# Attention-output transposes on half of the array, and eight other edits, in a kernel of sliding-window attention and RWKV channel mix

## Chip, cores and metric

One core of a Trainium2 chip runs the whole kernel. The metric is the device time of one launch in microseconds (us). Engines are named as in the profile: PE (TensorE matmul), PEld (its weight load), DVE (VectorE), ACT (ScalarE), POOL (GpSimd) and SP (SyncE). Lines such as L652 are lines of the kernel before.

## What is computed

```python
# q, k, v: (8, 8, 576, 64) f32: batch, heads, sequence, head size
scores = q @ k.T / 8
rel = pos[:, None] - pos[None, :]
mask = (rel >= 0) & (rel < 128)                    # window of 128, causal
attn = softmax(where(mask, scores - slope[h] * abs(rel), -1e9))   # slope[h] = 2**-(h+1)
x = (attn @ v) with the heads side by side         # (8, 576, 512)

xp = x moved down by one row, zeros in the first
xk = mu_k * x + (1 - mu_k) * xp
xr = mu_r * x + (1 - mu_r) * xp
v = relu(xk @ w_k) ** 2 @ w_v                      # w_k 512x1024, w_v 1024x512
out = sigmoid(xr @ w_r) * v                        # w_r 512x512, f32 result
```

## The kernel before

**A planner writes the order.** Every piece of work is added to a `Plan` (L33) as a node with an engine or a choice of engines, a duration from a formula, dependencies, buffers that it takes (`Hold`) and frees, and a priority. `Plan.run` (L89) plays these durations through and emits the instructions in the order that comes out. On the chip each engine then runs its own list strictly in that order. Attention work of group `g` of batch `b` is given the time `(4b + g - A[engine]) * SLOPE` in `rank` (L283), channel-mix work the sum of the PE time of the channel mix before it. So a larger `A` means that the engine takes attention earlier relative to the channel mix. `paced` (L742) holds back attention that would run too far ahead. `XRL` and `XD` delay the mixing of `xr` and of late batches.

**Attention.** The 8 batches have 4 groups of 2 heads each (a pair of heads is a group). For batches 1 to 4, q and k arrive as bf16 over POOL's DMA queue in `cb`, are transposed on PE (L935, eight 128x128 tiles) and copied from PSUM to `qk` by ACT. Batches 5 to 7 are transposed by DMA from SP's queue (L410) instead. `scores` (L531) multiplies q with k: the contraction is the 64 of the head size, so the two heads of a group sit in the upper and the lower 64 rows of the array, at the same time (12 matmuls at L559 for one group). ACT takes the exponential (L570), DVE multiplies by `mask` (L583), or, for the first groups, the bias is added by matmuls with `sid` and `dist` (L546). `attend` (L589) multiplies with v (18 matmuls at L614); DVE takes the reciprocal of the sums (L620) and normalizes into `xu` (L625). `out_t` (L641) transposes the five 128-row tiles of `xu` back on PE (L652, `xu` as the weights, the identity streaming through in 128 columns), and ACT copies 576 columns into `xt` (L529, the helper `copy_any`). `shift` (L661) makes the difference with the row before (L678) and mixes it into `xk` and `xr` (L685). Batches 6 and 7 go back by DMA (L697).

**Channel mix.** `channel_mix` (L750) works on at most 512 rows: eight blocks of `xk @ w_k` (L765), ReLU on ACT (L772), square on DVE or ACT (L738, L736), then, for each 128 rows, `xr @ w_r` (L783), tanh on ACT (L790), eight matmuls with `w_v` (L799), the product on DVE into one of four `ot` tiles (L804), and a DMA out from SP (L820). The last tile of all is done in column pieces of 384 and 128, both in one PSUM bank.

**Start.** Batch 0 is cut in two: `part` 0 is its first 256 rows, `part` 1 the rest. The f32 q and k of part 0 are loaded by six DMAs from SP (L422) into `stage`, cast to bf16 by ACT (L855), transposed on PE (L867) and copied to `qk` by ACT or DVE (L873). Part 1 and all the rest come over POOL's queue, casting, in the order `LOADS`: v tiles 0 and 1, half of `w_k`, k and q of part 1, the 64 rows at the end of q and k (`ts`, the tails), v tiles 2 and 3, the other half of `w_k`, batch 1, `w_r`, `w_v`. The tails are transposed at L716 and copied to `tt` by two DVE copies. `mask` is made by eight ACT exponentials (L900). 90 matmuls on zeros (L520) fill PE while there is nothing else to do.

**PSUM** has two double banks (`duo`, class `p2`) for scores and attention, and four single ones (`uno`, class `p1`) for everything else; the channel mix and the transposes share these four.

```python
A = {PE: 8.75, ACT: 4.50, DVE: 6.75, VIR: 0}
return {e: ((k - A[e]) * SLOPE,) + tuple(prio) for e in A}     # attention
return {e: (prio[1],) + tuple(prio) for e in A}                # channel mix
```

## Time and profile before

| | us |
|---|---|
| launch, median of 4 runs (lowest to highest) | 239.11 (238.65 to 240.27) |
| the profiled execution's own time | 238.65 |
| its span, first to last instruction | 236.9 |
| PE busy, of the span | 228.4 (96%) |
| DVE busy | 186.8 (79%) |
| ACT busy | 164.8 (70%) |
| POOL busy | 102.2 (43%) |
| `xt` copies of 576 columns on ACT, 20 of them, each | 0.647 |
| `mask` exponentials on ACT, 8 of them, each | 0.443 |

The profiled execution is also the fastest of the four; 1.75 us of its time lie outside the span. An engine's busy time says little by itself here, since matmul ends are modelled and shares are averages over a start, a long middle and an end; the prediction reads them by stretch. The granted TensorE clock is 1.00 in every stretch.

### The profile page before, as it was taken

To read this page: it belongs to the slowest core of one execution; us is meant where nothing else is said; L and a number is where in the kernel's file an instruction comes from. 1 tells how busy PE (TensorE), PEld (TensorE's weight loads), DVE (VectorE), ACT (ScalarE), POOL (GpSimd) and SP (SyncE) were. 2 spreads that over 40 slices of the span, in tenths; PEclk is the share of its full clock that TensorE was granted. 3 is DMA by queue.
4 is the path that set the end of the run, shared out by engine and by line. 5 is a ranking of instruction groups with operands and counts; after the bars stand their busy time and mean duration, and the time that the engine had idled before them with its cause. 6 is when DMAs were issued, how large, how long until landed. Compare 5 with 4: busy or idle time off the path is not lost.

```text
span 236.9 us, 5786 instructions
## 1 busy us (share of the span) xinstructions
PE 228.4 (96%) x2255; PEld 140.6 (59%) x2255; DVE 186.8 (79%) x420; ACT 164.8 (70%) x283; POOL 102.2 (43%) x128
## 2 busy tenths in 40 slices
PE   8969999999999999999999999999999999999993
PEld 7556676575675856565565674555565744455562
DVE  6676946899699998999999988975699955964342
ACT  4768999779998895977785776855783726326260
POOL 8778985598794893179257626000000000000000
PEclk9999999999999999999999999999999999999999
DMA  8999999999999999999999999972331214121212
GB/s 146 198 151 167 155 154 187 155 167 201 181 138 169 152 144 172 151 122 168 205 152 95 161 207 174 79 148 91 77 115 44 91 45 144 44 90 47 86 46 89
DMA packets 136491, 31.44 MB, mean 133 GB/s; under 512 B 127112, under 2 KB 131984, under 8 KB 136464
## 3 DMA queue, kind: packets, MB, share of 16 engines
q0 software_dynamic: 110992, 16.26, 110.9%
q1 hardware_dynamic: 25472, 14.82, 28.1%
q8 instruction: 17, 0.28, 0.5%
q14 instruction: 10, 0.08, 0.2%
HBM read 33.56 MB, written 9.44 MB: 182 GB/s over the span
## 4 chain that ended last, share of the span: by engine, by line
PE 84%; ACT 6%; DMA 4%; POOL 3%; issue 1%; DVE 0%; POOLq 0%; DVEq 0%; ACTq 0%
PE uno L799 27%; PE uno L765 25%; PE uno L783 13%; PE duo L614 7%; PE duo L559 6%; DMA ts<-in_k_dram 4%; PE uno L935 3%; PE uno L652 3%; POOL qx L381 1%; ACT at L570 1%; ACT qk L529 1%; ACT rl L772 1%; ACT xt L529 1%; PE uno L716 1%; ACT mask L900 1%
## 5 line engine op out<-in xcount | busy, mean ns | idle before, releaser
L799 PE MATMUL uno<-wv_sb,kk 128*128 128x512 bf16 (+2 forms) x296 | 72.1, 374 | 0.7 <-DVE ot L804 0.7
L570 ACT ACTIVATE at<-duo 128x1024 bf16<-128x1024 f32 (+2 forms) x68 | 65.3, 992 | 8.5 <-PE duo L559 8.5
L765 PE MATMUL uno<-xk,wk_sb 128*128 128x256 bf16 (+2 forms) x416 | 69.6, 314 | 0.2 <-ACT rl L772 0.2
L772 ACT ACTIVATE rl<-uno 128x256 bf16<-128x256 f32 (+2 forms) x104 | 47.9, 486 | 16.5 <-PE uno L765 14.8
L765 PEld LDWEIGHTS <-wk_sb 128*128 128x128 bf16 x416 | 38.9, 98 | 21.7 <-issue 0.3
L738 DVE TENSOR_TENSOR kk<-rl 128x256 bf16<-128x256 bf16 (+2 forms) x94 | 30.4, 339 | 15.5 <-ACT rl L772 14.4
L799 PEld LDWEIGHTS <-kk 128*128 128x128 bf16 x296 | 26.6, 98 | 26.4 <-issue 0.9
L384 POOL DMA_DIRECT2D vs<-in_v_dram x32 | 28.4, 901 | 27.2 <-PE duo L614 24.7
L790 ACT ACTIVATE rs<-uno 128x512 bf16<-128x512 f32 x36 | 22.2, 617 | 24.8 <-PE uno L783 24.6
L583 DVE TENSOR_TENSOR at<-at,mask 128x1024 bf16<-128x1024 bf16 x54 | 36.1, 678 | 4.1 <-ACT at L570 4.0
L783 PE MATMUL uno<-wr_sb,xr 128*128 128x512 bf16 x144 | 37.0, 379 | 0.0
L804 DVE SCALAR_TENSOR_TENSOR ot<-rs,uno 128x512 f32<-128x512 bf16 (+2 forms) x37 | 24.6, 666 | 14.1 <-PE uno L799 10.6
L406 POOL DMA_DIRECT2D cb<-in_k_dram x28 | 24.8, 897 | 9.1 <-DMA wv_sb<-in_moe_w_v_dram 4.1
L685 DVE SCALAR_TENSOR_TENSOR xk<-dl,mu_sb,xt 128x576 bf16<-128x576 bf16 (+2 forms) x36 | 26.7, 744 | 0.2
L406 POOL DMA_DIRECT2D cb<-in_q_dram x28 | 24.7, 906 | 4.5 <-PE uno L935 1.5
L685 DVE SCALAR_TENSOR_TENSOR xr<-dl,mu_sb,xt 128x576 bf16<-128x576 bf16 (+2 forms) x36 | 26.4, 743 | 0.0
L614 PEld LDWEIGHTS <-at 128*128 128x128 bf16 x576 | 21.9, 98 | 6.1 <-issue 0.3
L529 ACT COPY xt<-uno 128x576 bf16<-128x576 bf16 (+2 forms) x28 | 16.2, 582 | 9.2 <-PE uno L652 9.2
L783 PEld LDWEIGHTS <-xr 128*128 128x128 bf16 x144 | 13.5, 98 | 14.2
L529 ACT COPY qk<-uno 128x1024 bf16<-128x1024 bf16 (+1 forms) x20 | 18.1, 942 | 3.1 <-PE uno L935 2.7
L678 DVE TENSOR_TENSOR dl<-xt 128x576 bf16<-128x576 bf16 (+2 forms) x36 | 15.0, 422 | 5.3 <-ACT xt L529 4.9
L614 PE MATMUL duo<-vs,at 128*128 128x65 bf16 x448 | 19.1, 194 | 0.0
(64 smaller groups left out, 217.3 us busy)
## 6 DMA issues: line engine op xcount, KB each, us to landing
out_dram<-ot SPq DMA_DIRECT2D x35, 256.0 KB, 2.5
vs<-in_v_dram POOLq DMA_DIRECT2D x32, 128.0 KB, 6.5
cb<-in_q_dram POOLq DMA_DIRECT2D x28, 128.0 KB, 7.3
cb<-in_k_dram POOLq DMA_DIRECT2D x28, 128.0 KB, 6.5
wk_sb<-in_moe_w_k_dram POOLq DMA_DIRECT2D x2, 512.0 KB, 8.1
wv_sb<-in_moe_w_v_dram POOLq DMA_DIRECT2D x2, 512.0 KB, 10.6
ts<-in_q_dram POOLq DMA_DIRECT2D x8, 64.0 KB, 6.6
ts<-in_k_dram POOLq DMA_DIRECT2D x8, 64.0 KB, 6.5
```

The costliest lines, as they stand in the source:

```text
L384: return dma(POOL, 256, issue_t(1024), lambda e: nc.gpsimd.dma_start(out=vs_buf[h.idx][:, j, :, 0:D], in_=v[b, :, 128 * j:128 * j + 128].r ...
L406: return [dma(POOL, 256, issue_t(1024), lambda e, r=r: nc.gpsimd.dma_start(out=cb_buf[h.idx][:, i, r], in_=src[:, :, r]), [g]) for r in ra ...
L529: (nc.scalar.copy if e == ACT else nc.vector.tensor_copy)(out=out, in_=in_)
L570: lambda e, ah=ah, w=w, hp=hp: nc.scalar.activation(out=ah(), in_=two(hp)[:, :, 0:w], func=AF.Exp, scale=float(scale)), (), [hp])
L583: nc.vector.tensor_tensor(out=a, in0=a, in1=m, op=ALU.mult)
L614: nc.tensor.matmul(a[:, hl, t - t0], lhsT=at[:, lo:lo + 128], rhs=vs[:, u, 2 * g + hl, :] if u < NF else tvb[:, 2 * g + hl], start=(u == u ...
L685: lambda e: nc.vector.scalar_tensor_tensor(out=buf[hk.idx][:, g, e0 + c0:e0 + c1], in0=dls(), scalar=mu[:, g:g + 1], in1=xc(1), op0=ALU.mu ...
L738: nc.vector.tensor_tensor(out=out, in0=in_, in1=in_, op=ALU.mult)
L765: nc.tensor.matmul(one(hp)[:, 0:n], lhsT=wk_sb[:, po, 128 * fo:128 * fo + 128], rhs=xk_buf[hx.idx][:, po, c0:c1], start=(po == 0), stop=(p ...
L772: a = op(ACT, act_t(n), [s], pr, lambda e, hp=hp, hr=hr: nc.scalar.activation(out=rl_buf[hr.idx][:, 0:n], in_=one(hp)[:, 0:n], func=AF.Rel ...
L783: nc.tensor.matmul(one(hp), lhsT=xr_buf[hx.idx][:, po, 128 * c:128 * c + 128], rhs=wr_sb[:, po], start=(po == 0), stop=(po == NPO - 1))
L799: nc.tensor.matmul(one(hv)[:, a:b], lhsT=kk_buf[hk.idx][:, fo, o:o + 128], rhs=wv_sb[:, fo, a:b], start=(fo == 0), stop=(fo == NFO - 1))
```

## The change

What it does, part by part:

1. The transposes of the attention output of batches 1 to 5 (20 groups) use 64 of the 128 rows at a time: `out_some` instead of `out_t`. Each 128x128 tile becomes two weights of 64x128, one in each half of the rows, with 64 columns of the identity streaming; the two halves write to two PSUM banks, and two ACT copies (320 and 256 columns) take the place of one of 576. The transposes of q and k stay as they were (`QM = 0`).
2. The planner knows the cost of a change between 128-row and 64-row work on PE (`SWITCH`), takes 64-row work first while PE is in that mode (`pe_key`), and models the DMA queues in slices (`fab`).
3. A fifth `ot` tile (`NO = 5`); the early buffer `dl0` now lies in it.
4. The last tile's second column piece has a PSUM bank of its own, and its DMA goes out from ACT's queue. The seven tiles before the last are sent in two DMAs each (`n_split`).
5. Start: k of groups 0 to 3 is loaded from ACT's queue, q from SP's; groups 2 and 3 are transposed by PE in f32, straight from `stage`, without a cast; the casts of groups 0 and 1 go to DVE; the copies to `qk` go to ACT alone, batch 0's copies to `xt` to ACT or DVE. The first v load waits for k of group 0, and the causal cut of `dist` comes before it on POOL.
6. `mask` comes from eight PE matmuls and two ACT exponentials of 1024 columns.
7. The tails are copied to `tt` by one DVE copy of 512 columns, in a new order of columns.
8. All squares of the channel mix go to DVE.
9. Pacing: `A` from 8.75/4.50/6.75 (PE/ACT/DVE) to 10/3/5, `SLOPE` from 4.7 to 4.6, `XRL` from 3 to 4, `XD` from 4 to 7, `OTL` from 5 to 1.5.

```diff
+    SWITCH = 0.095
...
+    def pe_key(self, n, rows):
+        key = n.prio["PE"] if isinstance(n.prio, dict) else n.prio
+        if rows == 64 and n.rows[0] == 64:
+            return (-1e8,) + tuple(key)
+        if rows == 128 and n.lazy:
+            return (key[0] + self.wait,) + tuple(key[1:])
+        return tuple(key)
...
-                    cand.sort(key=lambda n: n.prio[e] if isinstance(n.prio, dict) else n.prio)
+                    if e == "PE":
+                        cand.sort(key=lambda n: self.pe_key(n, rows))
...
+                    if e == "PE":
+                        if n.rows[0] != rows:
+                            n.dur = dur = dur + self.SWITCH
+                        rows = n.rows[1]
...
-    XD = 4
-    OTL = 5.0
+    XD = 7
+    OTL = 1.5
...
-    NO = 4
+    NO = 5
+    WAIT = 0.0
+    QM = 0
+    OM = 1
...
-        return (DVE, ACT) if order < 3 else (DVE,)
-
-    XT0 = (ACT,)
-    QK0 = (ACT, DVE)
-    CAST = (ACT,)
+        return (DVE,)
+
+    XT0 = (ACT, DVE)
+    QK0 = (ACT,)
+    CAST = (DVE,)
+    FT = (2, 3)
+    KQ = ACT
+    VCUT = True
+    XTT = range(8, B)
+    MMASK = True
+    VDEP = 1
+    TCOST = 1.5
+    KLAST = 1
...
-    dl0 = cst.tile([128, H // 2, 256], BF16, name="dl0")
+    dl0 = ot_buf[NO - 1].bitcast(BF16).rearrange("p (g c) -> p g c", g=H // 2)
...
-    A = {PE: 8.75, ACT: 4.50, DVE: 6.75, VIR: 0}
+    A = {PE: 10.00, ACT: 3.00, DVE: 5.00, VIR: 0}
...
-    XRL = 3.0
+    XRL = 4.0
...
-    SLOPE = 4.7
+    SLOPE = 4.6
...
+        eng = KQ if i and g < 2 + KLAST else SPE
+        qe = nc.scalar if eng == ACT else nc.sync
...
+            return [put(155 * n, st[:, i], hs[:, 0:256].rearrange(
+                "h (p r) d -> p h (r d)", p=128))]
...
+        return [put(80 * n, st[:, i, r], hs[:, 128 * r:128 * r + 128].rearrange("h p d -> p h d"))
+                for r in range(2)]
...
+    if KQ == ACT:
+        plan.add(ACT, 1.28, 0.0, [last[ACT]], (-1e9,))
...
+            if what == "v" and VCUT:
+                n_w["d"] = pool_op(0.55, emit_cut, [n_ident])
             for j in ((0, 1) if what == "v" else (2, 3)):
-                vl[0].append(v_load(0, j, vh[0], [gv[0]] + blank_v))
-                if j == 0:
+                vl[0].append(v_load(0, j, vh[0], [gv[0]] + blank_v + (
+                    src0[1, VDEP - 1] if VDEP and j == 0 else [])))
+                if j == 0 and not VCUT:
...
+    def halves(n, block):
+
+        hp = [Hold("p1"), Hold("p1")]
+
+        def emit(e):
+            for i in range(n):
+                src, c = block(i)
+                for r in range(2):
+                    nc.tensor.transpose(
+                        one(hp[r]).bitcast(BF16)[:, c:c + 64], src[64 * r:64 * r + 64],
+                        ident[64 * r:64 * r + 64, 64 * r:64 * r + 64])
+
+        return hp, emit
+
+    def out_some(b, g, hx, deps, prio, ht):
+
+        m = len(hx)
+        hp, emit = halves(m * NJ, lambda i: (
+            xu_buf[hx[i // NJ].idx][:, i % NJ].rearrange("p h d -> p (h d)"), 64 * i))
+        o = op(PE, 0.0295 * m * NJ, deps, prio + (1,), emit, hp, hx)
+        o.rows, o.lazy = (64, 64), True
+        xs = []
+        for r in range(2):
+            nt = NJ - r
...
+            xs.append(op(XT(b, g), {ACT: act_t(64 * m * nt), DVE: dve_t(64 * m * nt)},
+                         [o, virt_xt[b]], prio + (1,), emit_c, (), [hp[r]]))
+        return xs
...
-        c = [op(DVE, dve_t(128), [t, g], prio + (0,), lambda e, j=j: emit_c(e, j), (), [hp])
-             for j in range(2)]
+        c = [op(DVE, dve_t(512), [t, g], prio + (0,), emit_c, (), [hp])]
...
+    n_hw = 39 + sum(4 if g in FT else 2 for g in range(3)) + 8 * len(XB) + len(XTT) + NJ * len(XO)
+    n_split = -n_hw % 8
...
             for a, b in ((0, FIN), (FIN, 512)) if final else ((0, 512),):
+                if a:
+                    hv = Hold("p1")
...
+                if a:
+                    y = plan.add(ACT, 0.4, 0.0, [d], (1e3,),
+                                 lambda e, ho=ho, row=row, a=a, b=b: nc.scalar.dma_start(
+                        out=of[row:row + 128, a:b], in_=ot_buf[ho.idx][:, a:b]))
+                else:
+                    def emit_s(e, ho=ho, row=row, a=a, b=b):
+                        cut = (a, 256, b) if 0 < B * S - 128 - row <= 128 * n_split else (a, b)
...
+                        if f32:
+                            nc.tensor.transpose(one(hp)[:, 128 * nn:128 * nn + 128],
+                                                staged(i, g, r), id32)
+                            continue
...
+    def mask_pe(j):
+        hp = Hold("p2")
+
+        def emit(e):
+            for h in range(4):
+                nc.tensor.matmul(two(hp)[:, h // 2, 256 * (h % 2):256 * (h % 2) + 256],
+                                 lhsT=sid[:, 4 * j + h], rhs=dist[:, 0:256],
+                                 start=True, stop=True, skip_group_check=True)
...
+            out=mask[:, 4 * j:4 * j + 4, 0:256],
+            in_=two(hp).rearrange("p b (h c) -> p (b h) c", h=2), func=AF.Exp,
+            scale=float(scale)), (), [hp])
...
-                xks[b, g], xrs[b, g] = out_t(b, g, 0, NJ, hx, [r], prio, xh[P], xth[b])
+                two_x.append((hx, r))
+                if len(two_x) < OM:
+                    continue
+                xs = out_some(b, g - OM + 1, [x for x, _ in two_x], [x for _, x in two_x], prio, xth[b])
```

## The prediction

> **What bounds the kernel now.** I read the page first, then busy time by stretch, then the chain of waits in order of time, in the middle, at the start and at the end.
>
> ```profile
> span 236.9 us, 5786 instructions
> PE   8969999999999999999999999999999999999993
> DVE  6676946899699998999999988975699955964342
> ACT  4768999779998895977785776855783726326260
> ```
>
> From the page: after the sixth slice (about 36 us) PE never leaves 9. DVE and ACT have slices of 9 too, so busy shares alone don't name the bound. The stretches show how close the others are:
>
> ```profile
> core 0: us, PE busy (x) PEld busy (x) DVE busy (x) ACT busy (x) POOL busy (x), PEclk, DMA share, GB/s
> 20.00:40.00 20.00, 18.88 (x249) 13.65 (x248) 13.12 (x37) 19.62 (x44) 15.73 (x19) 1.00 2.05 163
> 60.00:80.00 20.00, 20.00 (x247) 13.64 (x246) 18.14 (x36) 18.50 (x30) 14.79 (x18) 1.00 2.09 165
> 120.00:140.00 20.00, 20.00 (x219) 13.20 (x217) 19.32 (x43) 14.71 (x26) 12.59 (x15) 1.00 2.12 143
> ```
>
> In 20 to 40 us ACT is full and PE is not; afterwards PE is full, with DVE and ACT just under. A modelled PE end could hide idle time, so the chain is read piece by piece:
>
> ```profile
> 63.52 0.28 PE uno L652 x5
> 63.80 0.55 PE duo L559 x12
> 64.35 0.97 PE uno L783 x4
> 65.32 0.86 PE uno L799 x4
> ...
> 70.25 0.28 PE uno L652 x5
> 70.53 0.45 PE uno L935 x8
> ```
>
> Piece follows piece without a hole: four matmuls of 512 columns always take 0.86, five transposes 0.28 (0.056 each). Only PE work that goes away shortens this stretch. The first 512-column piece after a score burst takes 0.97: leaving 64-row work costs 0.11. The burst itself streams 1024 columns in each half of the array, 0.43 at 0.86/2048 per column, and takes 0.55: entering costs about 0.1 as well.
>
> At the start PE waits for a load, and at the end for DVE:
>
> ```profile
> 8.75 8.90 DMA ts<-in_k_dram
> 17.70 0.40 PE uno L716 x4
> ```
>
> ```profile
> 15.35 0.92 PE L867 MATMUL uno<-ident,qx 128*128 128x128 bf16 x13 [0.21 <-DMA qx<-in_k_dram]
> 17.70 0.40 PE L716 MATMUL uno<-ident,ts 128*128 128x128 bf16 x4 [1.43 <-DMA ts<-in_k_dram]
> ```
>
> ```profile
> 230.53 2.18 PE uno L799 x12
> ...
> 232.79 0.56 DVE ot L804
> ...
> 233.40 0.62 PE uno L799 x8
> ...
> 234.04 0.29 DVE ot L804
> ```
>
> The second of these fences is PE in order of time, with the idle time before a piece and what ended it in brackets: 1.43 us for the tails. The last is the end of the chain: the 128-column piece shares a bank with the 384-column one, so its matmuls wait until DVE has read that.
>
> **The change part by part.** The sum is made against the profiled execution, 238.65 (span 236.9 and 1.75 outside); the median of the runs, 239.11, stands 0.46 above it, which is added at the end.
>
> *The last piece, -0.7.* With its own bank the piece follows at 232.7 and ends by 233.3; DVE, done with the first product at 233.35, does the second by 233.65 instead of 234.33. SP's issue of the first piece (0.45 to 0.51 each at the start of the trace) would be in the way until 233.9, so ACT's queue is needed for that; ACT is idle there. No DMA of before comes from ACT, so its latency is unknown: -0.9 (as SP's) to 0 (0.7 later). I take -0.7, SP's row. Seven more issues on SP cost 3.5 us of a queue with about 2.5 us for each tile: hidden, +0.3 if the last but one tile's second half delays the last.
>
> *Half-array transposes, -1.8.* Removed: five at 0.056, 0.28 a group. Added: ten weights, ten matmuls of 64 columns. No such transpose is in the trace. The nearest row is the scores on `tt`, also 64 rows by 64 columns:
>
> ```profile
> L559 PEld LDWEIGHTS <-tt 64*128 64x128 bf16 x64 | 3.1, 94 | 0.0
> L652 PE MATMUL uno<-ident,xu 128*128 128x128 bf16 x120 | 11.3, 219 | 0.8 <-DVE xu L625 0.4 <-ACT qk L529 0.3
> ```
>
> 64 loads of 94 ns would be 6.0 in a row, yet their engine is busy for 3.1: the two halves load side by side, as the burst's time says of their matmuls. A pair should then cost about what one matmul of 65 columns costs at L614, 0.55/18 = 0.031; five pairs 0.15, a gain of 0.13 a group. The Trainium skill speaks against it ("TensorE: Matmul & The Clock Gate", LDWEIGHTS): a load's time is its columns over 1.2 GHz however few its rows, so 107 ns, and halves double the loads. By that, unhidden, five more loads cost 0.53 a group and the 20 groups get 8.1 slower (0.53 less 0.13). The trace already has 18 loads with their matmuls in 0.55, so the row decides. The mode change matters more: apart from a score burst, entering and leaving cost 0.2 and make 0.13 a loss of 0.07. In the PE list of before, 9 of the 20 `out_t` stand directly ahead of scores. All 20 beside scores: -2.6; nine: -0.4; none: +1.4. The product into `xu` frees the double bank for the next scores and readies the transposes at once, and the planner now prefers 64-row work in that mode: I take 16, -2.1 + 0.3. ACT pays two copies (0.466 and 0.374, by the 320- and 256-column rows) for one of 0.647, +0.19 a group: 60 to 80 us goes from 18.5 to 19.3 of 20. PE's next work covers this; without that cover it is 3.9 in all.
>
> *The start, -1.7.* Before 17.7 us PE has 1.43 idle and over 5 us of matmuls on zeros. Work that could stand there: the first four blocks of the channel mix, 16 matmuls of 256 columns at 3.06/28 = 0.109, 1.75 in all. They need the first half of `w_k` (issued at 3.85, median 8.1 to landing) and the last `xk` of part 0, done at 16.9 before. With k on ACT's queue beside q, k of group 0 can land near 2.9, where q does, instead of 3.9; groups 2 and 3 lose two casts of 0.40 each, the casts of groups 0 and 1 leave ACT, and the first scores no longer stand behind six load issues in a row. I put that `xk` at 15 to 15.5 and count 1.0 of the 1.75. From 20 to 40 us ACT is relieved: `mask` takes two exponentials of 1.045 instead of eight of 0.443 (-1.5), and three squares of 0.48 go to DVE, 13.12 of 20 busy. PE stalls of about 1.5 stand there (0.81 of it ahead of L935 at 29.95); I count 0.7. Bounds 0 and -3. Against it: four q/k copies move from DVE (0.69) to ACT (0.59), +2.4 on ACT before 17 us, where the casts (8 of 0.40) leave it.
>
> *Loads behind the new wait.* The first v load waits on POOL for k of group 0: about 1.4 becomes 3.1, less the cut (0.6) now ahead of it. Behind it on POOL stand v 1, `w_k`, four loads of part 1, the tails. `ts` was issued at 8.75 and landed 8.9 later, so it stood in the DMA queue, not in POOL's list; a shift of 1.2 is hidden while that holds. Zero; +1.2 if it doesn't.
>
> *f32 transposes, 0.* Eight; no f32 row of that size exists. Lower end: as bf16, 0. Upper: four passes ("FP8 and Floating Point Precision", TensorE Precision Notes, says that true FP32 takes four), 8 x 3 x 0.056 = +1.3. An estimate only, and covered by PE's idle time before 17.7; the page's price if that cover goes.
>
> *`mask` on PE, +0.5.* Eight matmuls of 256 columns, 0.87. They have the lowest priority and may fall into the stall at 29: 0 to +0.9. They hold a double bank that scores want.
>
> *At nothing:* the fifth `ot` (no wait of before has DVE waiting for an output DMA), `OTL`, and the tails' copy (one of 512 columns, 0.69 by that row, for two in 0.48: +0.2 of DVE a batch). The ten squares give DVE 3.2 more, seven of them after 40 us, where it is at 18.06 of 20; attention on DVE then slides towards 160 us and later, where DVE has 4 of 20 free. Without this slack the cost is those 3 us. Pacing itself moves order only; PE had one stall after 40 us, 0.7 near 53, so it can gain 0.7 and lose more. Zero.
>
> Sum: -0.7 - 1.8 - 1.7 + 0.5 = -3.7. 238.65 - 3.7 = 234.95; with the 0.46, 235.4.
>
> **The rivals.**
>
> *Banks (slower).* The half-array transposes hold two of the four single banks instead of one until two ACT copies are through, behind an exponential of 1.045: up to 1.9 us. "TensorEngine Tiling (Array Packing)", Gotcha 1, has the rule, that row tiles can't share a bank at one time; no row here shows it. The channel mix is left with two banks; a 256- or 384-column block holds one for 0.43 to 0.65 on PE, then ACT's wait and 0.40 to 0.52 of ReLU, some 1.3, so two banks just feed PE. A stall of 0.35 in each of 20 groups is +7.0: 242.4. It decides from 3.7/20 = 0.19 a group. For it: ACT and DVE above 18 of 20. Against: the longest ACT waits of before are for PE (`rs` 24.6, `rl` 14.8), not PE's for ACT, and the planner counts banks.
>
> *The start is hidden.* The loads set the start: tails at 17.65, v 2 and 3 and batch 1 after that, in the same order and volume. Then -1.7 is lost: 237.1.
>
> *Most of it fails to arrive.* The start hidden, and adjacency as before (-0.4 instead of -1.8): 238.5, no change that can be told.
>
> **How the numbers follow.** A difference of 0.5%, 1.2 us, is about what a measurement of this kernel can tell from none. Forecast 0.58 (235.4, own range 233.2 to 237.5 by the bounds of start and adjacency); start hidden alone 0.15 (237.1); most missing 0.12 (238.5); banks 0.15 (242.4). Faster by over 0.5% (below 237.9) 0.73, within 0.5% 0.12, slower 0.15. The range 233.2 to 239.0 takes in all but the slower case and a little at the low end.
>
> **What would show it.** Right: L652's successor at about 0.15 for ten, score bursts directly beside it in most groups; a channel-mix piece before 17.7; no idle time ahead of the last eight L799; ACT below 18.5 in 20 to 40. Wrong: PE pieces of the middle with idle time released by ACT or DVE; ten transposes near 0.3; `ts` later than 18.5; 0.97 after more bursts than the 28 of scores. Then the price of banks or of mode changes decides, and I have its sign wrong.

## The result and the profile after

The changed kernel takes 237.86 us (median of 43 runs, 236.91 to 239.11) against 238.87 for the kernel before (64 runs, 237.89 to 241.08, among them the four shown above). The ratio is 0.9951 with a 95% interval of 0.9938 to 0.9965: 0.5% faster, 1.2 us, where 3.7 had been forecast. The profiled executions say the same, 237.5 against 238.65.

Not all of the 1.2 us is work saved. Of 135 launches of the kernel before, timed beside the experiments, 24 have a mean granted clock of 0.993 or less and a median of 240.6 us (the others 238.69); of the changed kernel's 44 launches none is below 0.997. If the 16 of the 64 that took over 239.8 us are of this kind, as is likely (their clock isn't on record), 0.7 us are left without them. The last section shows what the clock does.

The page of after, the counterpart of the first lines shown of before:

```profile
span 235.7 us, 5995 instructions
PE   8899999999999999999999999999999999999993
DVE  7493966999787999999998999974789995984242
ACT  4649799659988978984986684938575826326260
```

PE still never leaves 9 after the sixth slice: it remains the bound, and the time gets shorter only by what PE no longer does or no longer waits for. By stretch (PE, PEld, DVE, ACT, POOL busy; clock; DMA), after:

```profile
20.00:25.00 5.00, 5.00 (x84) 3.14 (x82) 2.34 (x8) 4.46 (x10) 3.74 (x5) 1.00 2.21 165
25.00:30.00 5.00, 4.43 (x62) 3.52 (x59) 4.96 (x16) 4.08 (x10) 4.66 (x7) 1.00 2.37 149
30.00:40.00 10.00, 9.47 (x112) 7.06 (x112) 6.13 (x18) 10.00 (x19) 7.57 (x9) 1.00 1.81 175
60.00:80.00 20.00, 19.78 (x250) 13.11 (x249) 16.49 (x35) 18.30 (x32) 13.59 (x17) 1.00 2.15 158
120.00:140.00 20.00, 19.93 (x234) 12.46 (x232) 18.48 (x40) 14.62 (x30) 11.91 (x14) 1.00 1.50 133
```

and before, in the third of these stretches:

```profile
30.00:40.00 10.00, 9.80 (x117) 7.25 (x117) 4.99 (x14) 9.62 (x16) 6.85 (x9) 1.00 1.72 170
```

From 20 to 40 us ACT is relieved as forecast, by 1.1: the first three lines make 18.54, where it was 19.62. But PE is as busy there as before, 18.90 for 18.88, and from 30 to 40 us ACT is even fuller (10.00 for 9.62) and PE less busy. The ledger below finds 0.2 us less stall in the 20 us, where 0.7 was counted.

The chain in the middle shows the new transposes (L759) in both settings:

```profile
72.82 0.25 PE uno L759 x10
73.07 0.44 PE duo L646 x12
73.52 0.97 PE uno L929 x4
74.49 0.25 PE uno L759 x10
74.74 0.55 PE uno L1116 x8
```

Ten take 0.25 with the entry into 64-row work. Ahead of a score burst (L646) they pay the entry that the burst would have paid: the burst takes 0.44 instead of 0.55, so the group costs 0.14 where it cost 0.28. Ahead of 128-row work (L1116, eight 128-column transposes, 0.45 in other places) the exit comes on top: 0.35, a loss of 0.07. Both were forecast to 0.01. What wasn't is their number.

The start, in the chain of waits:

```profile
7.53 8.38 DMA qx<-in_k_dram
15.96 0.90 PE uno L1014 x13
...
17.89 0.33 PE uno L844 x4
18.22 0.87 PE uno L895 x8
```

The tails (L844) no longer have an idle stretch ahead of them, but PE now waits longer for part 1's k (L1014), which stands ahead of them in the queue and lands at 15.9: 0.56 us, for 0.21 before. The first channel mix (L895) stands behind both, at 18.2, not before 17.7 (by its first matmul at 18.06; it was 19.33 before, behind one more piece of scores).

The end, after, engine by engine (the bracket is the idle time before):

```profile
230.50 0.69 DVE L934 SCALAR_TENSOR_TENSOR ot<-rs,uno 128x512 f32<-128x512 bf16 x1 [2.80 <-PE uno L929]
231.22 1.50 SPq L959 DMA_DIRECT2D out_dram<-ot  x3
231.80 0.75 DVE L934 SCALAR_TENSOR_TENSOR ot<-rs,uno 128x384 f32<-128x384 bf16 x2 [0.61 <-PE uno L929]
232.58 0.37 ACTq L953 DMA_DIRECT2D out_dram<-ot  x1
```

The eight matmuls of the 128-column piece follow at once, and DVE does both products in one go until 232.55. But the span ends at 235.7, 3.2 later; before, it ended 2.6 after DVE. A DMA is in between, as the experiments show.

**The ledger.** I took all matmul starts of both traces in order. A matmul of N columns gets N/2400 + 0.0025 us, the line through the distances of starts at full clock (128 columns 0.0558, 512 columns 0.2158; four of 512 make 0.863, the 0.86 of the chain), or half of that in 64-row work, where two run side by side; each change between 64- and 128-row work gets 0.096 us; the rest is stall. Up to the start of the last 384-column piece, the forecast and the trace compare so (us, negative is faster):

| term | forecast | trace |
|---|---|---|
| start and ACT's relief, with `mask` on PE | -1.7 + 0.5 | -0.24: zeros 7.67 to 6.67, `mask` +0.87, stalls before 40 us -0.11 |
| half-array transposes | -1.8 | -1.13: work 6.70 to 4.04, changes 80 to 96 (+1.53) |
| stalls from 40 to 200 us | 0 | +0.38 (2.15 to 2.53) |
| last piece | -0.7 | -0.16: its start to the span's end, 5.646 to 5.484 |
| sum | -3.7 | -1.15 |

Sixteen more changes of mode are eight groups apart from scores at two each: 12 groups of 20 stand beside scores, not 16. Of the 1.0 that the zeros lose, 0.4 can't be put down to the change: the first zeros of both traces go by 0.107 apart, at half clock (the profile's clock column, which says 1.00 there, begins with the first full clock), until 6.4 us before and 4.5 after, and in the traces kept this moment lies anywhere from 4.0 to 10.0.

### The profile page after: what moved, and what is told of

It reads as the page before. It is cut to its first block, busy times and chain, and to the rows that moved or that the text cites. A ratio compares the mean times of both kernels' runs of the same rounds, so it can differ in the third digit from the quotient of the medians.

```text
span 235.7 us, 5995 instructions
## 1 busy us (share of the span) xinstructions
PE 228.2 (97%) x2363; PEld 138.2 (59%) x2363; DVE 188.0 (80%) x425; ACT 160.5 (68%) x280; POOL 102.6 (44%) x128
## 4 chain that ended last, share of the span: by engine, by line
PE 82%; ACT 7%; DMA 4%; POOL 3%; issue 2%; DVE 0%; DVEq 0%; POOLq 0%
PE uno L929 27%; PE uno L895 24%; PE uno L913 13%; PE duo L704 6%; PE duo L646 6%; DMA qx<-in_k_dram 4%; ACT rl L902 2%; PE uno L759 2%; ACT qk L616 2%; ACT at L660 2%; PE uno L1116 2%; POOL qx L430 1%; PE duo L633 1%; POOL vs L433 1%; PE uno L704 1%
## 5 line engine op out<-in xcount | busy, mean ns | idle before, releaser
L895 PE MATMUL uno<-xk,wk_sb 128*128 128x256 bf16 (+2 forms) x416 | 69.6, 314 | 0.4 <-ACT qk L616 0.3
L895 PEld LDWEIGHTS <-wk_sb 128*128 128x128 bf16 x416 | 38.7, 98 | 22.1 <-issue 1.4
L868 DVE TENSOR_TENSOR kk<-rl 128x256 bf16<-128x256 bf16 (+2 forms) x104 | 33.5, 337 | 15.9 <-ACT rl L902 14.5
L934 DVE SCALAR_TENSOR_TENSOR ot<-rs,uno 128x512 f32<-128x512 bf16 (+2 forms) x37 | 24.5, 667 | 14.5 <-PE uno L929 9.8
L616 ACT COPY xt<-uno 128x320 bf16<-128x320 bf16 (+1 forms) x45 | 16.0, 404 | 15.2 <-PE uno L759 12.5
L809 DVE SCALAR_TENSOR_TENSOR xk<-dl,mu_sb,xt 128x576 bf16<-128x576 bf16 (+1 forms) x32 | 24.8, 778 | 0.3
L809 DVE SCALAR_TENSOR_TENSOR xr<-dl,mu_sb,xt 128x576 bf16<-128x576 bf16 (+1 forms) x32 | 24.6, 774 | 0.0
L616 ACT COPY qk<-uno 128x1024 bf16<-128x1024 bf16 (+1 forms) x22 | 19.2, 929 | 1.9 <-PE uno L1014 1.3
L715 DVE TENSOR_TENSOR xu<-duo,rc 128x640 bf16<-128x640 f32 x20 | 16.4, 818 | 0.2
```

The costliest lines, as they stand in the source:

```text
L616: (nc.scalar.copy if e == ACT else nc.vector.tensor_copy)(out=out, in_=in_)
L809: lambda e: nc.vector.scalar_tensor_tensor(out=buf[hk.idx][:, g, e0 + c0:e0 + c1], in0=dls(), scalar=mu[:, g:g + 1], in1=xc(1), op0=ALU.mu ...
L868: nc.vector.tensor_tensor(out=out, in0=in_, in1=in_, op=ALU.mult)
L895: nc.tensor.matmul(one(hp)[:, 0:n], lhsT=wk_sb[:, po, 128 * fo:128 * fo + 128], rhs=xk_buf[hx.idx][:, po, c0:c1], start=(po == 0), stop=(p ...
```

## The experiments

Each kernel was timed beside the kernel before; ratios are to it, with 95% intervals. "To after" is the difference from 0.9951, times 238.87 us. Unless said otherwise the kernel is the changed one with one edit.

| kernel | ratio | interval | to after, us |
|---|---|---|---|
| e1, whole transposes, same order | 0.9984 | 0.9955 to 1.0014 | +0.8 |
| e2, transposes wait for 64-row mode | 1.0269 | 1.0206 to 1.0332 | +7.6 |
| e17, whole transposes, planned anew | 1.0032 | 1.0006 to 1.0058 | +1.9 |
| e4, last DMA from SP | 0.9940 | 0.9905 to 0.9974 | -0.3 |
| e5, before, own bank at the end | 1.0002 | 0.9982 to 1.0021 | |
| e3, old start | 1.0095 | 1.0058 to 1.0132 | +3.4 |
| e8, `mask` from ACT | 0.9952 | 0.9926 to 0.9979 | 0.0 |
| e11, tails loaded earlier | 0.9906 | 0.9877 to 0.9935 | -1.1 |
| e15, before, tails loaded earlier | 0.9952 | 0.9930 to 0.9974 | |
| e14, as e11, known to the planner | 0.9934 | 0.9907 to 0.9961 | -0.4 |
| e6, three squares on ACT again | 1.0017 | 1.0000 to 1.0035 | +1.6 |
| e7, old pacing | 1.0111 | 1.0091 to 1.0130 | +3.8 |
| e13, old start, squares and pacing | 1.0289 | 1.0247 to 1.0331 | +8.1 |
| e16, e13 with whole transposes | 1.0316 | 1.0267 to 1.0366 | +8.7 |
| e18, e16 with the old DMA model | 1.0031 | 0.9995 to 1.0067 | +1.9 |
| e9, `A` on PE 10.10 | 0.9975 | 0.9950 to 1.0000 | +0.6 |
| e12, `A` on DVE 5.25 | 0.9980 | 0.9955 to 1.0006 | +0.7 |
| e10, before, `A` on PE 8.85 | 0.9994 | 0.9967 to 1.0021 | |

### Transposes and banks

**e1** keeps the changed kernel's order on every engine and its two PSUM banks for each group, and transposes whole tiles again, three in one bank and two in the other:

```diff
-        hp, emit = halves(m * NJ, lambda i: (
-            xu_buf[hx[i // NJ].idx][:, i % NJ].rearrange("p h d -> p (h d)"), 64 * i))
+        hp = [Hold("p1"), Hold("p1")]
+
+        def emit(e):
+            for t in range(NJ):
+                nc.tensor.transpose(
+                    one(hp[t // 3]).bitcast(BF16)[:, 128 * (t % 3):128 * (t % 3) + 128],
+                    xu_buf[hx[0].idx][:, t].rearrange("p h d -> p (h d)"), ident)
...
```

> The changed kernel with every engine's order and both PSUM banks kept, but the five attention-output tiles of a group transposed whole again (five of 128 columns, three into one bank, two into the other; ACT copies of 384 and 192 columns). 80 mode changes on PE instead of 96. If the half-array transposes pay by their PE time alone (0.155 us instead of 0.28 for a group, and 0.096 us for each mode change, 12 groups beside scores and 8 apart), the time rises by 20 x 0.125 - 16 x 0.096 = 1.0 us. If they paid what the prediction put on them, it rises by 1.8. If the two banks are what costs, it stays within 0.3, since they are still held.

0.8 us slower than after, with an uncertainty of about 0.7. Its ledger has 80 changes of mode and 2.67 more work, so 1.13 was due. The half-array form is worth about 1, not 1.8, which lies outside that uncertainty. One thing differs from a pure test: e1's copies split the columns otherwise (384 and 192).

**e2** makes the planner hold the transposes back until PE is in 64-row mode:

```diff
-    WAIT = 0.0
+    WAIT = 60.0
```

> The changed kernel with WAIT = 60 instead of 0: half-array transposes give way to the channel mix while PE is in 128-row mode, so 18 of 20 stand beside scores instead of 12, and there are 84 mode changes instead of 96. By mode changes alone 12 x 0.096 = 1.15 us faster than the changed kernel (ratio to the kernel before about 0.990). If a later transpose starves the channel mix or the banks, the gain is eaten by PE stalls and the ratio is 0.995 or more.

Eighteen groups of 20 now stand beside scores and there are 84 changes of mode, 12 fewer, which are worth 1.15. The kernel is 7.6 slower: its stalls are 16.1 us instead of 8.2, 3.3 of them from 40 to 60 us and 3.7 at 195 to 198, where PE waits for the last batch's attention. The sixteen that I assumed can be had only by delaying the transposes, and what hangs on them costs far more. Part of the 7.6 is the clock, at 0.979 to 0.993 in five of six launches; the profiled one, at full clock, has a span 6.7 longer than after's.

**e17** goes back to the old transposes of one bank and one copy, and lets the planner plan with them (`OM = 0`).

> The changed kernel with whole transposes and one bank, planned as such (another order). Order kept, whole transposes were 0.8 us slower than the changed kernel. If the banks cost something in the changed kernel, a plan without the second bank gets some of the 0.8 back or more: ratio 0.993 to 0.997. If the order is worth what the nudges showed, 0.998 to 1.001. Above 1.005 if the numbers were fitted to the half-array transposes.

It is 1.9 slower than after. If the second bank cost what the rival said, 0.35 a group or 7 us, this kernel would have been some 6 faster, with the halves' 1.1 taken off. With e1, where the two banks stay and only PE's work differs, that refutes the bank rival. So does the ledger: from 40 to 200 us the stalls of after rose by 0.38 in all, which leaves no room for 7 us.

### The end

**e4** sends the last piece from SP's queue again, **e5** gives the kernel before nothing but the second bank, in its own order:

```diff
-                    y = plan.add(ACT, 0.4, 0.0, [d], (1e3,),
-                                 lambda e, ho=ho, row=row, a=a, b=b: nc.scalar.dma_start(
+                    y = plan.add(SPE, 0.6, 0.0, [d], (1, len(plan.nodes)),
+                                 lambda e, ho=ho, row=row, a=a, b=b: nc.sync.dma_start(
```

```diff
             for a, b in ((0, FIN), (FIN, 512)) if final else ((0, 512),):
+                if a:
+                    hv = Hold("p1")
...
```

> The changed kernel with the last column piece sent from SP's queue instead of ACT's, nothing else. The prediction counted ACT's queue as needed: then 0.1 to 0.3 us slower. If ACT's transfer is the slower one (1.92 us from issue to landing in the changed kernel, 1.55 from SP in the one before), up to 0.3 us faster.

> The kernel before with one edit: the last column piece has a PSUM bank of its own (its DMA still from SP); the order of every engine is the same. The prediction's step: 0.7 us faster (ratio 0.997). PE's idle time there was 0.86 by matmul starts in the trace of before. If the end is set by the output DMAs instead, as in the changed kernel, where PE ended 1.85 us earlier and the last landing 1.41, only 0.4 us (ratio 0.9985).

ACT's queue is worth nothing that shows, and, more surprising, neither is the bank: 1.0002, with an uncertainty of some 0.5 us, so that the 0.7 is out. The DMAs of e5's profile look like those of before at this place (KB each, median us from issue to landing), and its two products run as one, as in after:

```profile
out_dram<-ot SPq DMA_DIRECT2D x1, 192.0 KB, 1.9
```

```profile
234.80 0.75 DVE L804 SCALAR_TENSOR_TENSOR ot<-rs,uno 128x384 f32<-128x384 bf16 x2 [0.61 <-PE uno L799]
```

Counted from the start of the 384-column piece, the stations at the end are these:

| | before | after |
|---|---|---|
| last matmul | 2.55 | 1.69 |
| DVE done | 3.10 | 2.31 |
| landing of the 384-column piece | 3.99 | 4.01 |
| landing of the 128-column piece | 4.68 | 4.25 |
| span's end | 5.65 | 5.48 |

The last matmul is taken by its start; the landing at 4.68, which the trace doesn't give, is read from the end of SP's wait for it at 4.70. PE gains 0.86. The 192 KB of the first piece, issued at 2.14, land at 4.0 in both kernels, and the small piece can't end much before that: it lands at 4.25, from ACT's queue (issued 2.34) as from SP's (e4: issued 2.57, landed 4.24). So 0.43 of the 0.86 are left at the landing; the rest of the span behind it is 1.24 here for 0.97, and 0.16 remain. In the other kernels with the second bank the span ends at 5.15 to 5.48, so the gain of a single execution is 0.16 to 0.5; the median of e5 shows none. That the first piece's transfer holds up the second is read from these stations; a smaller first piece wasn't tried.

### The start

**e3** undoes the start: k on SP's queue, casts on ACT, no f32 transposes, the copies and the cut of `dist` as before, no wait of the first v load:

```diff
-    XT0 = (ACT, DVE)
-    QK0 = (ACT,)
-    CAST = (DVE,)
-    FT = (2, 3)
-    KQ = ACT
-    VCUT = True
+    XT0 = (ACT,)
+    QK0 = (ACT, DVE)
+    CAST = (ACT,)
+    FT = ()
+    KQ = SPE
+    VCUT = False
...
-    VDEP = 1
+    VDEP = 0
```

> The changed kernel with all edits of the start undone (k from SP's queue, no f32 transposes, casts on ACT, copies as before, first v load without wait, cut of dist after it); mask on PE, squares and the rest stay. If the start edits are worth the 1.7 us of the prediction, it is that much slower than the changed kernel (ratio to the kernel before about 1.002). If the loads set the start, it is within 0.4 us of the changed kernel (ratio 0.994 to 0.997).

3.4 us slower than after, which looks as if the new start were worth twice its forecast. The profile says otherwise. Its clock (after POOL's column) is below 1 at the start:

```profile
0.00:17.70 17.70, 14.84 (x165) 11.55 (x166) 9.53 (x46) 8.48 (x16) 12.77 (x22) 0.90 1.55 164
```

It is 0.5 from 9.60 to 13.02 us, after PE waited 1.76 for a load of v, and in 8 of the 12 launches the mean clock is 0.993 or less. The other four launches have a median of 240.16, 2.3 above after; so about a third of the 3.4 is the clock. And from 30 to 40 us PE is busy 8.16 of 10, where the kernel before, with the same start, has 9.80: the old start is bad under the new pacing. What it is worth by itself can't be read from this run. I return to that below.

**e8** makes `mask` on ACT again (`MMASK = False`).

> The changed kernel with the mask from eight ACT exponentials again instead of eight PE matmuls and two exponentials. PE does 0.87 us less, ACT 1.5 more. If PE's work counts, 0.5 to 0.9 faster (prediction: +0.5 for the edit, so 0.5 faster without it, but the start's ACT relief lost again, 0.7 of which half is the mask's). If ACT bounds 20 to 40 us, it is slower by 0.5 to 1.5.

No difference (uncertainty some 0.6): `mask` on PE is worth and costs nothing that shows. Its 0.87 of PE are paid back by zeros and waits that they take the place of, as the ledger's first row says.

**e11** tests what the chain shows, that loads set the start. The first half of `w_k` is issued after batch 0's tails and part 1's k and q instead of before them; every engine's other order stays:

```diff
...
-        for n in plan.run():
+        order = [n for n in plan.run() if n is not moved["k"]]     # first half of w_k
+        order.insert(order.index(moved["t"]) + 1, moved["k"])      # behind the tails
+        for n in order:
```

> The changed kernel with the order of all engines kept, but on POOL's queue the first half of w_k is loaded after the tails of batch 0 instead of before part 1 of q and k. Part 1 and the tails should land about 2 us earlier (k of part 1 at 13.5 to 14 instead of 15.9, tails at 15.5 instead of 17.5), w_k at about 17.5, just ahead of its first use at 18.05; batch 1 lands as before, at 29.4. If the tails' load alone holds the start back, 1 us or more faster. If batch 1's loads bind what follows, whatever is gained at 16 us is idle again by 30 us: within 0.4 us of the changed kernel.

0.9906, the fastest kernel of all: 1.1 us (uncertainty some 0.8) ahead of after, 2.2 ahead of before. In its trace the tails land at 14.5 instead of 17.5, part 1's k at 13.3 instead of 15.9, and batch 1's last k at 28.8 instead of 29.4. The profiled executions differ by 0.56 only, 235.7 and 235.2 us of span, nearly all of it before 20 us, so the rest of the 1.1 isn't seen in a trace. What binds the start now is another load, the second of v, and from its landing to 28.2 us PE's own list, with no idle time over 0.02 in the profile:

```profile
3.24 6.24 DMA vs<-in_v_dram
9.48 0.04 issue
9.52 0.43 PE uno L708 x9
...
12.58 1.40 PE uno L611 x25
13.98 0.11 PE uno L746 x2
14.09 1.00 PE uno L611 x18
...
17.53 0.33 PE uno L848 x4
17.86 0.87 PE uno L899 x8
```

The first channel mix comes 0.36 earlier only. The zeros (L611) are in the way themselves, since their number and their places are fixed in PE's list: `xu` was ready at 13.48 and 14.55, and its transposes (L746) begin at 13.81 and 14.93, behind zeros. In the trace of before such a transpose starts 0.06 after `xu`, so I estimate that the zeros cost 0.6 us here, and as much in after, where the waits are the same. Part 1's transposes, whose data lie there from 13.3, start at 15.3 behind them. A kernel with fewer zeros wasn't run. **e15** does the same to the kernel before.

> The kernel before with the same swap of loads and every engine's order kept. PE waits there for the tails (1.43 us at 17.7), and part 1's k lands at 15.3. If loads set its start, 0.8 to 1.4 us faster (ratio 0.994 to 0.9965), as much as the whole change brought. If batch 1's loads (28.9) bind anyway, within 0.4 us.

0.9952: as much as the whole change. The order of two loads is worth about 1.1 in either kernel, and the change had left that order as it was. Here too a part is the clock: none of its 12 launches is below 0.996, and against the launches of before above 0.993 (median 238.69) its median of 237.78 is 0.9 faster. **e14** tells the planner of the new order (`LOADS = 'v23tKVkabcRWw'`), so that the engines' orders move too.

> The changed kernel with the order of loads of the swapped one (part 1 of q and k and the tails ahead of the first half of w_k), but known to the planner, which may write another order for all engines. If the load order itself carries the 1.1 us, as fast as the swapped one (ratio 0.989 to 0.992); a new order of the plan may add 0.6 us, as the nudges did (0.993 to 0.994).

0.4 ahead of after and within the uncertainty of both it and e11. A new plan isn't better than the old one with the loads swapped.

### Squares, pacing and the planner

**e6** lets ACT take squares of the first three orders again, **e7** restores the old pacing numbers:

```diff
-        return (DVE,)
+        return (DVE, ACT) if order < 3 else (DVE,)
```

```diff
-    XD = 7
-    OTL = 1.5
-    A = {PE: 10.00, ACT: 3.00, DVE: 5.00, VIR: 0}
-    XRL = 4.0
-    SLOPE = 4.6
+    XD = 4
+    OTL = 5.0
+    A = {PE: 8.75, ACT: 4.50, DVE: 6.75, VIR: 0}
+    XRL = 3.0
+    SLOPE = 4.7
```

> The changed kernel with the squares of the first three parts of the channel mix on DVE or ACT again, as before. If moving them to DVE relieved ACT in the start, as the prediction had it, undoing it is slower by 0.3 to 0.7 us. If the planner only fills ACT with other work, it is within 0.3 us of the changed kernel (ratio 0.994 to 0.9965).

> The changed kernel with the pacing of before (A, SLOPE, XRL, XD, OTL). The prediction put the pacing at zero: within 0.5 us of the changed kernel. If the new pacing cost what was gained at the start (PE stalls of 40 to 150 us rose from 1.9 to 2.3, and ACT is full in 30 to 40 us), it is 0.5 to 1.5 us faster. If start edits and pacing belong together, it is slower by 1 us or more, as with the old start in the changed kernel. 102 mode changes instead of 96 add 0.6.

1.6 and 3.8 slower than after, where I had put both at nothing. With e3 that makes 8.8 us for three undone parts of a change that brings 1.2. **e13** undoes all three at once. If they only fit each other, it should come near the kernel before; if they add, near +8.8.

> The changed kernel with the start edits, the squares and the pacing all undone together (each alone was slower than the changed kernel: 3.4, 1.6 and 3.8 us); half-array transposes, mask on PE, own bank of the last piece and the planner's new rules stay. If the three are worth what each alone showed, the sum makes it 5 us or more slower than the changed kernel (ratio 1.015 or more). If they only fit each other and are worth nothing as a block, it is within 0.6 us of the changed kernel (ratio 0.993 to 0.998).

They add: +8.1. Yet the start, squares and pacing of e13 are those of the kernel before, which doesn't have these 8 us. Something else in the changed kernel must make them bad. **e16** asks whether it is the transposes and their banks, by taking those back as well (`OM = 0`).

> As the joint undo (start, squares and pacing of before in the changed kernel), and the transposes of the attention output whole again with one bank, planned as such. If the two banks and the preference for 64-row work are what made the joint undo 8 us slower, most of it goes: ratio 1.008 or less. If the other rules of the planner (durations of tails' loads, sliced DMA queues, earlier release of output tiles) do it with the old numbers, it stays at 1.02 or more.

It is not: +8.7. What is left is the planner's picture of the machine. **e18** is e16 with the old model of the DMA queues:

```diff
-                        cand.sort(key=lambda n: (n.queue == served, n.base.t0, n.seq))
+                        cand.sort(key=lambda n: n.prio)
...
-    TCOST = 1.5
+    TCOST = 1.0
...
-        m = max(1, round(us / 0.25))
+        m = 1
...
-        return fab(queue, kb / RATE, n, lat, free)
+        x = fab(queue, kb / RATE, n, lat, free)
+        x.prio = (len(plan.nodes),)
+        return x
```

> As the joint undo with whole transposes, and the planner's model of the DMA queues as before (one slice for each transfer, in program order, tails' loads at their plain size). If the sliced DMA model is what makes the old numbers bad, ratio 1.01 or less. If it is the PE rules (switch cost, shorter scores) or several together, 1.02 or more, and the cause within the planner stays open.

6.8 us go: 1.0031, the level of the kernel before. So the new model of the DMA queues, with the old numbers, makes a poor order. That the new start, squares and pacing mainly repair this is the likely reading, but it isn't shown: the changed kernel with the old model wasn't run. From 60 to 80 us, e13 and then e18:

```profile
60.00:80.00 20.00, 18.98 (x239) 12.19 (x237) 16.16 (x30) 17.86 (x33) 15.08 (x18) 0.85 2.14 129
```

```profile
60.00:80.00 20.00, 19.84 (x220) 12.98 (x222) 17.40 (x33) 18.19 (x30) 17.65 (x22) 1.00 2.26 168
```

PE's clock, 0.85 and 1.00 here, is part of it, and is told at the end.

**e9, e10 and e12** move one pacing number slightly, to see how much the order alone moves the time:

```diff
-    A = {PE: 10.00, ACT: 3.00, DVE: 5.00, VIR: 0}
+    A = {PE: 10.10, ACT: 3.00, DVE: 5.00, VIR: 0}     # e9
+    A = {PE: 10.00, ACT: 3.00, DVE: 5.25, VIR: 0}     # e12
-    A = {PE: 8.75, ACT: 4.50, DVE: 6.75, VIR: 0}
+    A = {PE: 8.85, ACT: 4.50, DVE: 6.75, VIR: 0}      # e10, in the kernel before
```

> The changed kernel with A for PE at 10.10 instead of 10.00: the same work, 98 mode changes instead of 96 (+0.2), but the planner writes another order from the middle of the attention on. If undoing squares, pacing or start was slower because of what those edits are, a nudge of 1% should be within 0.4 us of the changed kernel (ratio 0.995 to 0.997). If the planner's order itself is what the changed kernel's numbers were fitted to, it is slower by 1 us or more.

> The kernel before with A for PE at 8.85 instead of 8.75: the same work and mode changes, another order. Within 0.4 us of the kernel before if the order matters little; slower by 1 us or more if the numbers of before were fitted to its own order as well.

> The changed kernel with A for DVE at 5.25 instead of 5.00: the same work in another order, 98 mode changes. The same two readings as for the nudge of PE: within 0.4 us, or slower by 1 us or more if the order was fitted.

Half of after's lead over before goes with either nudge (+0.6, +0.7); before's own time hardly moves (-0.1). Each of these is about as large as its own uncertainty, and 0.2 of it are two more changes of mode; together they make it likely that some 0.6 us belong to the particular order, not to any part of the change.

## Why the prediction was wrong

- **The bound** was read rightly. PE is the bound before and after, and the ledger of PE's time adds up to the difference of the profiles.
- **The start (-1.7 + 0.5 forecast, -0.24 measured) is the step that failed first,** with 1.0 of the 2.5 us that the sum is off. The argument was that the first `xk` hangs on k of group 0, and the first channel mix on that `xk`. K of group 0 landed at 3.6 instead of 3.9, not at 2.9, and q later, at 3.3 instead of 2.9. But part 0's attention also needs the second load of v, and that landed at 9.3, 0.4 later than before; PE waited for it, and from there to 15.4 ran without a hole, 53 zeros included. Part 0's last `xk` was done at 16.3, not 15 to 15.5. And the channel mix didn't follow `xk`: in PE's list it stands behind part 1's transposes, which waited for their k until 15.9, and the tails. The change doesn't move these loads in POOL's queue. Moving them brought the first channel mix forward by 1.3 in the kernel before (e15, 19.33 to 18.05) and by 0.4 in the changed one (e11); what remains there is v's load and PE's list.
- **ACT's relief (0.7 of the 1.7)** came, 1.1 us from 20 to 40 us, and bought 0.2: PE's stalls there go from 2.4 to 2.2. PE's three longest waits there end with single pieces, `xu` on DVE (0.37) and ACT's copies to `xt` (0.27) and `qk` (0.31): what counts is when these come in their engine's list, not how full ACT is in 20 us.
- **The half-array transposes (-1.8 forecast, -1.1 by the ledger, -0.8 by e1).** The price was right: 0.14 beside scores, 0.35 apart. The weight rule that spoke against them (the Trainium skill, "TensorE: Matmul & The Clock Gate", LDWEIGHTS), 107 ns a load, would have made it over 1 us for the ten by my estimate; 200 loads of 95 ns are busy for 4.1 us, so the two halves load side by side, as those of the scores do:

```profile
L759 PEld LDWEIGHTS <-xu 64*128 64x128 bf16 x200 | 4.1, 95 | 7.5 <-DVE xu L715 1.7 <-issue 1.7 <-DVE dl L802 1.3
```

  The term that was mis-sized is the count: 16 groups beside scores assumed, 12 found. e2 shows that 18 can be had, and at what price.
- **The last piece (-0.7 forecast, -0.16).** I followed PE, DVE and the issue, and stopped there. Next late is the landing of the larger first piece, which starts no earlier than before; e5, with no gain in its median, agrees.
- **`mask` on PE** was put at +0.5 net of the start's cover; e8 says 0. **f32 transposes at 0**: seven ran in 0.98, from 7.75 on, after 0.83 of waiting for q,

```profile
7.75 0.98 PE L1011 MATMUL uno<-id,qx 128*128 128x128 f32 x7 [0.83 <-DMA qx<-in_q_dram]
```

  so they cost some 0.11 each, twice a bf16 one and half of the four passes that I had as the upper end ("FP8 and Floating Point Precision", TensorE Precision Notes); the time was PE's to spare, as said.
- **Loads behind the new wait**: zero held (the tails landed at 17.5 for 17.7), but there is no such wait on the chip. It is in the planner's times alone: in the trace POOL issues the first v load at 2.22, right behind the cut, 1.4 us before k of group 0 lands. Not at 3.1, as I had it.
- **Pacing and squares at zero** was right only as a net, and by luck: the prediction didn't have the reason. Not one of them is without effect (e6, e7); most likely they make up for what the new DMA model does to the order (e18). This cancels in the time of after, up to the 0.4 of stalls.
- **The rivals.** Banks: refuted (e1, e17). The start hidden: held in its outcome and half in its mechanism, since v's load and the zeros in PE's list bind as well. "Most of it fails to arrive" (238.5) is nearest to what happened, though its count of transposes was too low. What none of them had was the last piece's landing, and the launches of before at a lower clock.

Open: why e3, e6 and e7, each alone, lose 1.6 to 3.8. That the DMA model is behind their sum is shown (e16, e18); which transfer times of the model mislead the planner wasn't tried. Of e11's 1.1 the traces show 0.56.

## What to carry to other kernels

Where one engine is full, sum its own work, its mode changes and its stalls from instruction starts, and believe a saving on another engine only if something waits for that. Look at the granted clock of every launch before you credit a difference to an edit. Of a saving at the very end, follow the last bytes to their landing: an earlier, larger transfer may be the one that ends last. Parameters of a planner fit its model, so undoing one part measures the fit and not the part's worth; undo the model too, and nudge a number to see what the order by itself is worth.

## What the runs showed of the hardware

**PE's clock can halve on a low share of work, without a long gap, and it changes on a grid of 3.41 us.** In e13 PE is busy for little of 54 to 60 us, and its clock then halves (the last three columns are clock, DMA share and GB/s):

```profile
54.00:56.00 2.00, 1.30 (x19) 1.03 (x17) 1.60 (x4) 2.00 (x5) 1.38 (x3) 1.00 1.96 222
56.00:58.00 2.00, 0.79 (x12) 0.57 (x12) 1.86 (x3) 2.00 (x4) 2.00 (x3) 1.00 1.97 226
58.00:60.00 2.00, 1.08 (x22) 1.01 (x22) 1.74 (x5) 2.00 (x3) 0.91 (x2) 0.81 2.30 163
60.00:62.00 2.00, 1.70 (x32) 1.37 (x30) 1.65 (x5) 0.79 (x2) 1.93 (x3) 0.50 2.42 154
64.00:66.00 2.00, 2.00 (x8) 0.97 (x7) 1.96 (x4) 1.70 (x4) 1.73 (x3) 0.50 2.76 151
66.00:67.00 1.00, 1.00 (x10) 0.43 (x9) 1.00 (x2) 0.69 (x2) 1.00 (x2) 0.96 3.84 128
```

PE was busy 3.17 us of those 6, with 1.43 as its longest single wait:

```profile
57.07 0.34 PE L646 MATMUL duo<-qk 64*128 64x256 bf16 x4 [0.52 <-ACT at L660]
...
58.91 0.74 PE L704 MATMUL duo<-vs,at 128*128 128x65 bf16 x15 [1.43 <-DVE xr L809]
...
63.61 3.32 PE L895 MATMUL uno<-xk,wk_sb 128*128 128x384 bf16 x12
```

In the last row 384-column matmuls go by at about 0.32 each until 66; at full clock they take 0.163 (384/2400 + 0.0025). The Trainium skill ("TensorE: Matmul & The Clock Gate", What's actually happening) puts the switch to half speed after an idle window of about 3.4 us. No gap of that length is in this trace, so a thin window is enough.

The clock fell in the middle of four traces: at 59.25 us in e13, 58.19 in e16, 9.60 in e3 and 18.36 in e5 (there after 1.06 of waiting for part 1's k). Counted from the moment at which each trace first has full clock (4.63, 6.99, 6.19 and 4.70), these are 16, 15, 1 and 4 times 3.413 us to within 0.01, and the half clock lasted two of these windows in e13 and e16, one in e3 and e5. In the window before the fall PE was busy for 33, 51, 46 and 46% of it. In all the other windows between the first full clock and 230 us, of all 20 traces, the lowest share that left the clock at 1.00 is 45%, in e2 at 198.6 us. So in these runs the limit lies near one half, counted by window and not by gap (busy times are modelled, so no closer than that). In the profiled execution of before the thinnest 3.41 us, with PE busy for 1.42, begin at 14.29, across a boundary of this grid at 16.67, and the clock stays. Since the first full clock lies elsewhere in each execution, the same waits can cost some launches their clock and not others; that this is what happens in the 24 launches is likely, but none of them was traced.

From 60 to 66 us in e13 PE was busy for 5.2 at half speed, 2.6 us of work lost, about a third of its 8.1: stalls close to each other cost more than their sum. The same happens in e16 and not in e18.

**A mode change costs about 0.1 us each way**: by matmul starts 0.096 into 64-row work and 0.107 out of it, before and after, and back-to-back half-array work pays it once. **A second queue for k slowed q**: issued at the same time as q from ACT's queue, group 0's k landed 0.3 sooner and its q 0.5 later.
